# General pass in steps of 128 tokens, cut into finer parts; the first q block by rows; the second group's weight maxima later

## The chip, the cores and the metric

One core of a Trainium2 chip runs the whole program. Its engines are TensorE (PE in the rows, PEld its weight loads), VectorE (DVE), ScalarE (ACT), GpSimd (POOL) and SyncE (SP), whose queue issues nearly all the transfers. The metric is the device time of one execution in microseconds; the median of three runs is compared.

## The reference, cut to what matters

```python
# attention over pooled keys, four batches of 12288 tokens, 128 channels
kv_pool = kv.reshape(B, H // 4, 4, W // 4, 4, C).mean(axis=(2, 4))
k = v = kv_pool.reshape(B, -1, C) @ w_sr              # 768 keys per batch
s = (q @ k.transpose(0, 2, 1)) / np.sqrt(C)
a = np.exp(s - s.max(-1, keepdims=True))
x = (a / (a.sum(-1, keepdims=True) + 1e-9)) @ v
# top-1 mixture of 8 experts, 128 -> 1024 -> 128
logits = x @ w_gate
e = argmax(logits)                                     # per token
y = np.maximum(x @ w1[e], 0) @ w2[e] * softmax(logits)[e]
```

q is drawn with a standard deviation of 0.8, the other inputs are small, so that within a batch nearly all tokens choose the same expert.

## The kernel before, in words

The tokens go in 96 blocks of 512 (24 per batch), in groups of four blocks (the first group of batch 0 has two). For a block the kernel takes scores in four tiles of 128 tokens (`scores`: six matmuls, a row maximum `nmax` on VectorE, the exponential `a` on ScalarE, a split into two f16 halves `ah`, a DMA transpose to `aT`), then the values (`values`, 18 matmuls), the split `xh`, `xl`, and the logits. For a group it counts votes and takes the expert that most tokens chose; all its blocks run through that expert. The expert part has eight slices `f` of the hidden layer: three matmuls into a PSUM bank (`hidden_sum`), the relu `hh` on ScalarE, the rest `hl` on VectorE, which frees the bank, and three slices later the three matmuls into `y` (`combine`). A product is always the sum of three with split operands.

A token that chose another expert than its group isn't covered. `code` notes it, `left` counts such tokens by (batch, expert), and a general pass serves them: `count_steps` turns the counts into steps of TAIL tokens, and `tail_step` is one step for one (batch, expert) list. It works out which list and which part of it (`u`, `li`), loads that expert's weights and that batch's keys and values, counts the list's tokens along each partition (`hit`, `tab`), finds the rows of each tile of 128 (`sel`, `row`, `v`, `at`), gathers their q rows by an indirect DMA, splits the weights, and then runs scores, values, gate and the expert part on TAIL columns; `tail_rows` writes the rows back by one indirect DMA per tile. With TAIL = 256 a step has TC = 2 tiles. Two steps (EXTRA) are placed between the last block but one and the last block; a loop at the end would run further ones. `tail_step` is a generator: it yields between its parts, and `search()` advances every running step by one part; it is called once behind each slice `f` of the last blocks (`m_`). A second step starts when the first has set `found`.

Most of the program is ordered by hand. `at(time, part, ...)` puts a part on a list by a due time in units near a microsecond, `beside(t, c, ...)` hangs one on the score matmuls of block t, tile c, and `run` emits the parts in the order of their times; each engine works through its own parts in that order. The first eight blocks have a shorter plan (`plan_short`, SHORT = 9.8 a block), the others LEN = 18.7, with the expert part LAG = 8 blocks behind. `plan_group` places a group's gate and votes and `plan_weights` its weights: `scales_part` advances `weight_scales` (two maxima over the weights on VectorE, `ws` L407, a matmul, then the scales), `split_part` the f16 halves. The second group has its own branch (`t < LAG`). The last eight blocks and the general steps stand outside this: they are written in program order, of which the framework may depart.

At the start `kv_load` issues four transfers for each of six key tiles, `first_keys` pools them (`pooled` on VectorE, eight matmuls that add the other half on TensorE), projects them and, at the last tile but one, prepares the first block's q: it was loaded in 32-column pieces (`q_load`, four transfers), turned on VectorE in blocks of 32 x 32 (`q_turn`), copied to `qh` on ScalarE, with the rest `ql` on VectorE.

Of the kernel before, what the change touches and what calls it, by code (L numbers as in the profile page):

```python
# [10 lines left out]
F32 = mybir.dt.float32  # L11
# [8 lines left out]
P = 128  # L20
# [10 lines left out]
TINY = 1e-30  # L31
TAIL = 256
EXTRA = 2
# [5 lines left out]
def attention_moe(ctx: ExitStack, tc, q, kv, w_sr, w_gate, w1, w2, out, tail=True):  # L39
    nc = tc.nc  # L40
# [6 lines left out]
    KT = NK // P  # L47
# [480 lines left out]

    def q_prep(t):
        q_turn(t)  # L530
        q_high(t)
        q_low(t, nc.vector)

    pending, waiting, searches = [], [], []
# [200 lines left out]
    def tail_step(job, aside=False):  # L735
# [6 lines left out]
        nc.vector.tensor_mul(le, le, ends)  # L742
        nc.vector.tensor_reduce(u[:, 1:2], le, axis=AX.X, op=ALU.max)
        nc.vector.tensor_sub(u[:, 1:2], step, u[:, 1:2])
        nc.vector.tensor_scalar_mul(u[:, 1:2], u[:, 1:2], float(TAIL))
# [20 lines left out]
        nc.vector.tensor_scalar(hit[:, :NJ], code, u[:, 2:3], None, op0=ALU.is_equal)  # L766
        nc.vector.tensor_tensor_scan(tab[:, :NJ], hit[:, :NJ], hit[:, :NJ], 0.0, op0=ALU.add, op1=ALU.max)
        nc.vector.tensor_copy(tab[:, NJ + 1:NJ + 2], part)
        nc.vector.memset(tab[:, NJ + 2:NJ + 3], 1.0)
        yield  # L770
        yield
        cnt = tab[:, NJ - 1:NJ]
# [8 lines left out]
        for c in range(TC):  # L781
# [11 lines left out]
            row = one.tile([P, NJ + 3], F32, name="row")  # L793
            nc.vector.tensor_copy(row, pr[:, :NJ + 3])

            nc.vector.tensor_scalar(v[:, 2:3], part, u[:, 1:2], float(c * P), op0=ALU.add, op1=ALU.add)
# [18 lines left out]
        for _ in weight_scales(raw, to, bank):  # L815
            pass
        ws = to[0]
        for _ in split_expert(raw, ws, w, 0, aside):
            pass
        yield  # L820
        for _ in split_expert(raw, ws, w, 1, aside):
            pass
        job["found"] = True
        yield
        pq = bank()
# [21 lines left out]
        job["x"] = x = xh, x_low(po, k, TAIL, xh)  # L847
        yield
        yield
# [35 lines left out]
    raws = {}  # L885
    for t in range(KT):
        raws[t] = kv_load(0, t)
        if t == KT - 3:
            q_load(0, nc.sync)
    q_load(1, nc.sync)  # L890
    gate_weights()

    def first_keys():

        for t in range(KT):
            kv_pool(0, t, raws.pop(t))
            pt = bank()[:, :P]
            k = KEYS[0]
            own = k.pop(("pooled", t))
            parts = k.pop(("parts", t))  # L900
            for i, part_ in enumerate(parts):
                mm(pt, part_, ident, i == 0, False)
            if t > 0:
                kv_project(0, t - 1, bank()[:, :P])
                kv_high(0, t - 1)
            mm(pt, own, ident, False, True)
            k["pt"] = pt
            kv_turned(0, t)
            if t > 0:
                kv_low(0, t - 1)  # L910
            if t == KT - 2:
                q_prep(0)
        kv_project(0, KT - 1, bank()[:, :P])
# [123 lines left out]
    def plan_group(g, t):  # L1037

        if t < LAG:

            T = LAG * LEN
            group_gate(g)
            for _ in range(6):
                at(T + 3.5, gate_part, g)
# [6 lines left out]
            at(T + 15.0, gate_part, g)  # L1051
            return plan_weights(g, t + 1)
        T = t * LEN
# [16 lines left out]

    def plan_weights(g, t):
        T = t * LEN
        at(T + 17.1, scales_part, g)
        T += LEN
        at(T + 0.7, scales_part, g)
        beside(t + 1, 1, scales_part, g)
        at(T + 5.8, scales_part, g)
        at(T + 6.8, gate_part, g)
        at(T + 6.85, gate_part, g)
        at(T + 9.25, split_part, g, 0)  # L1080
        at(T + 14.95, split_part, g, 0)
# [200 lines left out]
```

## Time and profile before

| | |
|---|---|
| median of 3 runs (lowest, highest) | 1928.78 us (1925.33, 1931.13) |
| profiled execution: time, span | 1929.05 us, 1927.3 us |
| TensorE busy | 1875.2 us (97%) |
| VectorE busy | 1419.7 us (74%) |
| ScalarE busy | 1306.2 us (68%) |
| GpSimd busy | 1365.6 us (71%) |
| mean granted clock of TensorE | 0.994 of full speed |

The shares are means over stages with different limits. A matmul's busy time overlaps its neighbours', so the distance between two starts is the better measure of what one costs.

### The profile page before, as it was taken

Reading aid. Unit: us, or ns where it says so; the run is one execution under the profiler, and the core shown is the slowest. Engines: PE = TensorE matmul, PEld = TensorE weight load, DVE = VectorE, ACT = ScalarE, POOL = GpSimd, SP = SyncE. Lnnn points to the kernel's source line nnn. Section 1 sums busy time; section 2 is a strip of 40 time slices with the busy share of each in tenths; the row PEclk is TensorE's granted clock in tenths of the full one; section 3 lists DMA queues with packets and bytes.
Section 4 is the critical chain, followed back from the end, with each engine's and each line's share of the span. In section 5 each row is a group of like instructions: output and inputs, shape, how many; then the busy total and the mean of one; then the engine's idle time right before and its main releaser. Section 6 shows DMA issues by size and latency. Waiting matters only on the chain.

```text
span 1927.3 us, 30394 instructions
## 1 busy us (share of the span) xinstructions
PE 1875.2 (97%) x9950; PEld 1095.0 (57%) x9950; DVE 1419.7 (74%) x2774; ACT 1306.2 (68%) x2376; POOL 1365.6 (71%) x1395
## 2 busy tenths in 40 slices
PE   6889999999999999999999999999999999999987
PEld 5655555555555555555555555555555555555444
DVE  5777787877787787776777777767767767767685
ACT  2777767766776766766767767767667677677454
POOL 1778688668878867867778787678677677776253
PEclk8999999999999999999999999999999999999999
DMA  6888989769987976887878777877867777776432
GB/s 163 164 165 160 186 168 174 145 126 191 177 165 152 189 146 123 172 153 130 178 156 173 167 152 143 157 136 159 147 129 143 150 126 147 143 135 132 112 95 46
DMA packets 1001409, 287.85 MB, mean 149 GB/s; under 512 B 905984, under 2 KB 983938, under 8 KB 1001248
## 3 DMA queue, kind: packets, MB, share of 16 engines
q1 hardware_dynamic: 1000992, 285.79, 75.2%
q8 instruction: 79, 1.29, 0.3%
q14 instruction: 82, 0.67, 0.1%
q0 software_dynamic: 256, 0.10, 0.0%
HBM read 81.34 MB, written 30.15 MB: 58 GB/s over the span
## 4 chain that ended last, share of the span: by engine, by line
PE 88%; DVE 4%; DMA 3%; issue 2%; POOL 1%; ACT 1%; SPq 1%; POOLq 0%; DVEq 0%; ACTq 0%
PE m L131 44%; PE y L131 25%; PE s L131 20%; DVE hl L460 1%; DMA aT<-ah 1%; DMA kv_raw<-in_kv_dram 1%; POOL ah L338 1%; SPq L173 0%; DMA aT<-in_kv_dram 0%; DVE nmax L309 0%; ACT a L313 0%; ACT hh L454 0%; DVE ws L407 0%; DMA kv_raw<-in_moe_w_dram 0%; DMA yT<-y 0%
## 5 line engine op out<-in xcount | busy, mean ns | idle before, releaser
L338 POOL TENSOR_TENSOR ah<-a,ah 128x768 f16<-128x768 f32 x381 | 626.0, 1647 | 313.0 <-ACT ah L336 297.8
L454 ACT ACTIVATE hh<-m 128x512 f16<-128x512 f32 (+1 forms) x784 | 462.6, 591 | 412.3 <-PE m L131 410.6
L460 DVE SCALAR_TENSOR_TENSOR hl<-m,hh 128x512 f16<-128x512 f32 (+1 forms) x784 | 532.7, 681 | 227.6 <-ACT hh L454 199.2
L131 PE MATMUL s<-k_sb,qh 128*128 128x384 f32 x1552 | 469.9, 383 | 4.7 <-ACT a L313 4.5
L313 ACT ACTIVATE a<-s,nmax 128x768 f32<-128x768 f32 x388 | 350.5, 903 | 125.9 <-DVE nmax L310 104.9
L309 DVE TENSOR_REDUCE nmax<-s 128x1 f32<-128x768 f32 x388 | 369.6, 953 | 68.2 <-PE s L131 60.0
L131 PE MATMUL m<-aT,v_sb 128*128 128x512 f16 (+1 forms) x1656 | 383.6, 377 | 1.6 <-DVE hl L460 1.6
L131 PEld LDWEIGHTS s<-k_sb,qh 128*128 128x128 f32 x1552 | 288.0, 190 | 61.7 <-ACT a L313 6.7
L131 PE MATMUL m<-xh,w1h 128*128 128x512 f16 (+1 forms) x776 | 296.3, 382 | 13.0 <-DVE hl L460 10.3
L131 PE MATMUL y<-hh,w2h 128*128 128x512 f16 (+1 forms) x776 | 293.6, 378 | 1.8 <-ACT y L483 1.8
L131 PE MATMUL y<-hl,w2h 128*128 128x512 f16 (+1 forms) x776 | 293.9, 379 | 0.0
L131 PE MATMUL y<-hh,w2l 128*128 128x512 f16 (+1 forms) x776 | 293.9, 379 | 0.0
L131 PE MATMUL m<-xl,w1h 128*128 128x512 f16 (+1 forms) x776 | 293.7, 378 | 0.0
L131 PE MATMUL m<-xh,w1l 128*128 128x512 f16 (+1 forms) x776 | 293.4, 379 | 0.0
L131 PEld LDWEIGHTS <-v_sb 128*128 128x128 f16 x1764 | 170.9, 98 | 204.3 <-issue 3.8
L131 PE MATMUL s<-k_sb,ql 128*128 128x384 f32 x776 | 262.8, 339 | 0.6 <-DVE ql L295 0.6
L131 PEld LDWEIGHTS <-w2h 128*128 128x128 f16 x1552 | 151.5, 98 | 184.0 <-issue 6.7
L334 POOL CAST ah<-a 128x768 f16<-128x768 f32 x187 | 154.3, 825 | 85.6 <-ACT a L313 80.7
L131 PEld LDWEIGHTS <-w1h 128*128 128x128 f16 x1552 | 124.6, 100 | 136.6 <-issue 62.0
L336 ACT CAST ah<-a 128x768 f16<-128x768 f32 x194 | 161.9, 834 | 9.5 <-issue 3.6
L354 DVE SCALAR_TENSOR_TENSOR xl<-m,xs,xh 128x512 f16<-128x512 f32 (+1 forms) x92 | 68.6, 745 | 129.2 <-ACT xh L349 127.3
L527 POOL TENSOR_TENSOR ql<-qT,qh 128x512 fp32r<-128x512 f32 x95 | 120.9, 1272 | 48.5 <-ACT qh L522 48.3
(214 smaller groups left out, 2087.7 us busy)
## 6 DMA issues: line engine op xcount, KB each, us to landing
kv_raw<-in_moe_w_dram SPq DMA_DIRECT2D x54, 512.0 KB, 4.7
q_sb<-in_q_dram SPq DMA_DIRECT2D x384, 64.0 KB, 2.5
out_dram<-o SPq DMA_DIRECT2D x96, 256.0 KB, 2.3
kv_raw<-in_kv_dram SPq DMA_DIRECT2D x84, 256.0 KB, 4.6
aT<-ah SPq DMA_TRANSPOSE x381, 3.8
aT<-in_kv_dram SPq DMA_DIRECT2D x12, 256.0 KB, 7.4
k_dram<-k_sb SPq DMA_DIRECT2D x8, 384.0 KB, 3.1
v_dram<-v_sb SPq DMA_DIRECT2D x8, 192.0 KB, 2.6
```

What stands on the lines that cost most here:

```text
L131: nc.tensor.matmul(o, l, r, start=start, stop=stop)
L309: nc.vector.tensor_reduce(nmax, pss[:, :, :KH], axis=AX.XY, op=ALU.max, negate=True)
L313: nc.scalar.activation(a.rearrange("p (h k) -> p h k", h=2), pss[:, :, :KH], AF.Exp, bias=nmax, scale=1.0, accum_out=sums)
L334: nc.gpsimd.tensor_copy(ah[:, 0], a)
L336: nc.scalar.copy(ah[:, 0], a)
L338: nc.gpsimd.tensor_sub(ah[:, 1], a, ah[:, 0])
L354: nc.vector.scalar_tensor_tensor(xl[:, :n], po[:, :n], k["xs"][:, 0:1], xh[:, :n], op0=ALU.mult, op1=ALU.subtract)
L454: nc.scalar.activation(hh[:, :n], ph[:, :n], AF.Relu)
L460: nc.vector.scalar_tensor_tensor(hl[:, :n], ph[:, :n], 0.0, hh[:, :n], op0=ALU.max, op1=ALU.subtract)
L527: by.tensor_sub(ql, BL[t].pop("qT"), qh)
```

## The change

TAIL becomes 128, so a general step has one tile. `tail_step` yields at other places: more often among its first VectorE instructions, after each part of the weights' maxima and of their split, and no longer at places where nothing was done. The first block's q is loaded by whole rows in one transfer, ahead of the last key tile, turned by four TensorE transposes into a PSUM bank, and split from there. For the second group the first part of the gate is placed earlier, and the two weight maxima and what follows them later.

```diff
--- before.py
+++ after.py
@@ -29,7 +29,7 @@
 W1_TOP = 2.0 ** 5
 W_TOP = 2.0 ** 14
 TINY = 1e-30
-TAIL = 256
+TAIL = 128
 EXTRA = 2
 SQ = 32
 FAR = 1.0e6
@@ -526,11 +526,6 @@
         qh, ql = BL[t]["qhl"]
         by.tensor_sub(ql, BL[t].pop("qT"), qh)
 
-    def q_prep(t):
-        q_turn(t)
-        q_high(t)
-        q_low(t, nc.vector)
-
     pending, waiting, searches = [], [], []
     OTHERS = {}
 
@@ -741,6 +736,7 @@
         nc.vector.tensor_reduce(u[:, 0:1], le, axis=AX.X, op=ALU.add)
         nc.vector.tensor_mul(le, le, ends)
         nc.vector.tensor_reduce(u[:, 1:2], le, axis=AX.X, op=ALU.max)
+        yield
         nc.vector.tensor_sub(u[:, 1:2], step, u[:, 1:2])
         nc.vector.tensor_scalar_mul(u[:, 1:2], u[:, 1:2], float(TAIL))
         nc.vector.tensor_scalar_add(u[:, 2:3], u[:, 0:1], 1.0)
@@ -765,10 +761,9 @@
         nc.vector.tensor_scalar(below, slot, part, None, op0=ALU.is_gt)
         nc.vector.tensor_scalar(hit[:, :NJ], code, u[:, 2:3], None, op0=ALU.is_equal)
         nc.vector.tensor_tensor_scan(tab[:, :NJ], hit[:, :NJ], hit[:, :NJ], 0.0, op0=ALU.add, op1=ALU.max)
+        yield
         nc.vector.tensor_copy(tab[:, NJ + 1:NJ + 2], part)
         nc.vector.memset(tab[:, NJ + 2:NJ + 3], 1.0)
-        yield
-        yield
         cnt = tab[:, NJ - 1:NJ]
         pb = bank()
         mm(pb[:, :1], below, cnt, True, True)
@@ -792,6 +787,7 @@
             mm(pr[:, :NJ + 3], sel, tab[:, :NJ + 3], True, True)
             row = one.tile([P, NJ + 3], F32, name="row")
             nc.vector.tensor_copy(row, pr[:, :NJ + 3])
+            yield
 
             nc.vector.tensor_scalar(v[:, 2:3], part, u[:, 1:2], float(c * P), op0=ALU.add, op1=ALU.add)
             nc.vector.tensor_sub(v[:, 2:3], v[:, 2:3], row[:, NJ:NJ + 1])
@@ -813,15 +809,12 @@
         w = job["w"] = []
         to = []
         for _ in weight_scales(raw, to, bank):
-            pass
+            yield
         ws = to[0]
-        for _ in split_expert(raw, ws, w, 0, aside):
-            pass
-        yield
-        for _ in split_expert(raw, ws, w, 1, aside):
-            pass
         job["found"] = True
-        yield
+        for i in range(2):
+            for _ in split_expert(raw, ws, w, i, aside):
+                yield
         pq = bank()
         for c in range(TC):
             nc.tensor.transpose(pq[:, c * P:(c + 1) * P], q_sb[:, c, :], ident)
@@ -846,7 +839,6 @@
         xh = x_high(po, k, TAIL)
         job["x"] = x = xh, x_low(po, k, TAIL, xh)
         yield
-        yield
         lg = one.tile([P, TC, E], F32, name="lg_t", bufs=2)
         logits_sum(logits(x, TC, bank()), lg)
         to = []
@@ -884,9 +876,11 @@
 
     raws = {}
     for t in range(KT):
+        if t == KT - 1:
+
+            q0 = two.tile([P, CH, C], F32, name="q_sb")
+            nc.sync.dma_start(q0, q[0, :BLK].rearrange("(c p) d -> p c d", p=P))
         raws[t] = kv_load(0, t)
-        if t == KT - 3:
-            q_load(0, nc.sync)
     q_load(1, nc.sync)
     gate_weights()
 
@@ -909,7 +903,10 @@
             if t > 0:
                 kv_low(0, t - 1)
             if t == KT - 2:
-                q_prep(0)
+                pq = bank()
+                for c in range(CH):
+                    nc.tensor.transpose(pq[:, c * P:(c + 1) * P], q0[:, c, :], ident)
+                BL[0]["qhl"] = q_halves(pq, CH, nc.vector)
         kv_project(0, KT - 1, bank()[:, :P])
         kv_high(0, KT - 1)
         kv_low(0, KT - 1)
@@ -1040,7 +1037,8 @@
 
             T = LAG * LEN
             group_gate(g)
-            for _ in range(6):
+            at(begin(LAG - 1) + 4.64, gate_part, g)
+            for _ in range(5):
                 at(T + 3.5, gate_part, g)
             at(T + 6.1, group_count, g)
             beside(LAG, 2, group_votes, g)
@@ -1049,7 +1047,7 @@
             at(T + 12.35, gate_part, g)
             at(T + 12.4, group_left, g)
             at(T + 15.0, gate_part, g)
-            return plan_weights(g, t + 1)
+            return plan_weights(g, t + 1, True)
         T = t * LEN
         group_gate(g)
         at(T + 6.8, gate_part, g)
@@ -1068,16 +1066,16 @@
         at(T + 15.0, gate_part, g)
         plan_weights(g, t + 1)
 
-    def plan_weights(g, t):
+    def plan_weights(g, t, late=False):
         T = t * LEN
-        at(T + 17.1, scales_part, g)
+        at(T + (18.9 if late else 17.1), scales_part, g)
         T += LEN
-        at(T + 0.7, scales_part, g)
-        beside(t + 1, 1, scales_part, g)
-        at(T + 5.8, scales_part, g)
+        at(T + (5.8 if late else 0.7), scales_part, g)
+        beside(t + 1, 2 if late else 1, scales_part, g)
+        at(T + (11.4 if late else 5.8), scales_part, g)
         at(T + 6.8, gate_part, g)
         at(T + 6.85, gate_part, g)
-        at(T + 9.25, split_part, g, 0)
+        at(T + (11.55 if late else 9.25), split_part, g, 0)
         at(T + 14.95, split_part, g, 0)
         at(T + 16.8, split_part, g, 0)
         at(T + 18.9, split_part, g, 1)
```

`q_halves`, which the new lines call, copies the PSUM bank to `qh` on ScalarE and subtracts it to `ql` on the engine that it is given.

## Rows read from the trace of the kernel before

**Rows 1.** The page: span, and the queue of the indirect transfers (packets, MB, share).
```profile
span 1927.3 us, 30394 instructions
...
q0 software_dynamic: 256, 0.10, 0.0%
```

**Rows 2.** Busy time of each engine by stage; then granted clock, DMA share, GB/s.
```profile
150.00:1790.00 1640.00, 1640.00 (x8683) 947.75 (x8681) 1215.96 (x2300) 1150.18 (x2082) 1232.58 (x1258) 1.00 0.79 153
...
1816.00:1860.00 44.00, 34.31 (x149) 15.84 (x148) 40.80 (x112) 24.57 (x39) 24.27 (x29) 0.97 0.56 164
...
1882.00:1906.00 24.00, 20.11 (x148) 13.88 (x147) 16.28 (x42) 14.69 (x34) 12.05 (x12) 1.00 0.36 78
1906.00:1918.00 12.00, 11.65 (x59) 5.58 (x56) 6.41 (x11) 5.41 (x10) 3.02 (x3) 1.00 0.02 5
```

**Rows 3.** SyncE's queue of transfers near the start, in order of time.
```profile
13.94 3.66 SPq L514 DMA_DIRECT2D q_sb<-in_q_dram  x4
```

**Rows 4.** All engines where the first keys end, in order of time.
```profile
31.12 0.69 DVE L527 TENSOR_TENSOR ql<-qT,qh 128x512 fp32r<-128x512 f32 x1 [0.69 <-ACT qh L522]
...
31.73 1.88 DVE L181 TENSOR_REDUCE pooled<-kv_raw 128x128 f32<-128x1024 f32 x1
...
34.82 0.60 PE L131 MATMUL s<-k_sb,qh 128*128 128x384 f32 x2
...
35.10 0.28 ACT L218 ACTIVATE k_sb<-m 128x128 fp32r<-128x128 f32 x1 [0.58 <-PE m L131]
...
35.57 0.29 DVE L224 SCALAR_TENSOR_TENSOR k_sb<-m,k_sb 128x128 fp32r<-128x128 f32 x1 [1.57 <-ACT vT L219]
```

**Rows 5.** TensorE around the second group; brackets give the wait and what ended it.
```profile
123.70 0.38 PE L131 MATMUL m<-xh,w1h 128*128 128x512 f16 x1 [1.48 <-DVE hl L460]
...
138.11 0.38 PE L131 MATMUL m<-xh,w1h 128*128 128x512 f16 x1 [2.33 <-DVE lg L367]
```

**Rows 6.** VectorE in the same stretch.
```profile
118.69 1.10 DVE L379 TENSOR_SCALAR gate<-sums 128x16 f32<-128x16 f32 x1
...
136.12 1.22 DVE L407 TENSOR_REDUCE ws<-kv_raw 128x1 f32<-128x1024 f32 x1 [2.31 <-DMA kv_raw<-in_moe_w_dram]
```

**Rows 7.** TensorE groups by shape, 1815 to 1928 us.
```profile
L131 PE MATMUL m<-vT,sel 128*128 128x387 f32 x8 | 4.1, 602 | 0.1
```

**Rows 8.** The chain that ended last: six score matmuls of a general step.
```profile
1851.79 1.06 PE s L131 x6
```

**Rows 9.** TensorE in the second general step: neighbouring 256-column matmuls.
```profile
1905.00 0.27 PE L131 MATMUL m<-xl,kv_raw 128*128 128x256 f16 x1
1905.11 0.27 PE L131 MATMUL m<-xh,kv_raw 128*128 128x256 f16 x1
```

**Rows 10.** TensorE in a logits stretch: neighbouring pairs, each with its weight load.
```profile
1793.96 0.17 PE L131 MATMUL m<-wg,xh 128*128 128x16 f16 x1
1793.98 0.17 PE L131 MATMUL m<-wg,xl 128*128 128x8 f16 x1
```

**Rows 11.** Who waited for whom on TensorE, 1790 to 1928 us: total, times, longest.
```profile
PE m L131 <- DVE hl L460: 11.4, 12, 4.0
```

**Rows 12.** VectorE groups by shape, 1815 to 1928 us.
```profile
L786 DVE TENSOR_TENSOR v<-v,vT 128x1 f32<-128x1 f32 x4 | 2.3, 585 | 0.0
...
L806 DVE TENSOR_SCALAR at<-v 128x1 int32<-128x1 f32 x4 | 0.6, 149 | 0.1
```

**Rows 13.** All engines at the end, in order of time.
```profile
1916.81 0.97 POOL L871 DMA_INDIRECT out_dram<-o,at  x1 [4.64 <-DVE o L500]
...
1919.02 0.69 DVE L500 TENSOR_TENSOR o<-m,cover 128x512 f32<-128x512 f32 x1 [2.49 <-PE m L498]
1919.15 0.97 POOL L871 DMA_INDIRECT out_dram<-o,at  x1 [1.37 <-DMA out_dram<-o,at]
1923.03 0.37 SPq L721 DMA_DIRECT2D out_dram<-o  x1
```

**Rows 14.** Busy time by stretch after the longest wait of the tail.
```profile
1857.00:1864.00 7.00, 6.02 (x14) 2.37 (x14) 4.99 (x11) 1.19 (x2) 2.71 (x3) 0.52 0.59 114
```

## Prediction

> **What bounds the kernel now.** I read the stages first. From 150 to 1790 us TensorE is busy for all 1640.00 of 1640.00 us [rows 2], and the diff changes nothing that is issued there; so this stretch keeps its length and only slides with whatever ends before it. What can move lies at the two ends. In the tail, from 1816 on, the picture turns: between 1816 and 1860 VectorE is busy 40.80 of 44 us and TensorE only 34.31 [rows 2], so there the search of the general steps on VectorE sets the pace. The waits of TensorE say how: 12 waits of 11.4 us in all end at `hl`, the longest 4.0 us [rows 11]; `hl` frees the PSUM bank that the next hidden matmul needs, and it stands on VectorE's queue behind pieces of the search. From 1882 to 1918 TensorE works 20.11 + 11.65 of 36 us [rows 2]: short waits, mostly its own work. At the start the transfer queue and VectorE's order decide, and near 136 us one stall can be read off directly.
>
> **Is the number of steps the same?** A step serves one (batch, expert) list. The indirect queue moved 0.10 MB in both directions [rows 1]; at 512 B a row that is at most 0.105 MB / 2 / 512 B, about 103 rows each way, pad rows not moved. So no list can hold more than 128 rows, every list that fitted one step of 256 fits one of 128, and the closing loop, of which the trace shows no pass, stays empty. Both placed steps remain, at half the width.
>
> **The yields.** I counted the calls of `search()` that a step needs: before, 12 to `found` and 26 to the end; after, again 12 and 26. A step begins and ends at the same places of the block program; only the work inside is cut finer. The weight load moves from the second call to the third and its maxima from the eleventh to the ninth, six calls later instead of nine; a call comes once per part of a block, six 512-column matmuls of twice 0.109 us [rows 9], so six calls are some 8 us. If the load is issued late all the same, the maximum waits in front of an `hl`, as it does for 2.31 us near 136 [rows 6], and TensorE behind it; I leave that to the range.
>
> **Tail, TensorE.** Two 256-column matmuls start 0.109 us apart [rows 9]. No 128-column f16 matmul with its own weight load stands in the trace. Bounds: 0.109 (no gain) and 0.02, at which pairs of 8 and 16 columns start, each behind a weight load [rows 10]. I take half, 0.055, since 256 columns are five times as slow as the floor and columns therefore set the pace. Per step 48 matmuls of the expert and 18 of the values shrink: 2 x 66 x 0.054 = 7.1 us. One score tile per step goes, 1.06 each [rows 8]: 2.1. One `sel` matmul pair per step goes: four tiles took 4.1 us busy [rows 7], overlapped, so 0.8 each: 1.6. The turns of q and of the output and the logits of the second tile, a few tenths: 0.3. Sum 11.1 us. Against it: one f takes six matmuls, 0.33 us, nearly what ScalarE (0.28) and VectorE (0.29) need for 128 columns [rows 4]; TensorE no longer covers them with ease, so I give back 1.0 (bounds 0 and 3). Net 10.1.
>
> **Tail, VectorE.** Twelve groups make one tile's search; their means, from 585 ns down to 149 [rows 12], sum to 4.96 us. One tile per step disappears, 9.9 us over both steps, besides a row maximum each. TensorE's waits between 1816 and 1860 are 44 - 34.31 = 9.7 us [rows 2]; with the search's clumps halved and the two weight maxima and the split no longer in one piece, I take 3.0 of them back (bounds 0 and 9.7): part of a removed clump only uncovers the wait for ScalarE. Behind the longest wait the granted clock was 0.52 for 7 us [rows 14], so TensorE's 6.02 us there were near its lower level, 1.2 GHz, and would have taken about 3.1 at 2.4; if that wait falls short, up to 2.9 returns. I take 1.2.
>
> **The end.** Now two indirect writes of the last step follow each other, and the last block's output waits for both: its data are ready at 1919.02 + 0.69 = 1919.71, its transfer is issued at 1923.03 [rows 13], 3.3 us later. The second write started 2.34 behind the first, at 1919.15, and the output 3.88 behind the second [rows 13]: a write takes 2.3 to 3.9 us to land. A single one from 1916.81 lands between 1919.1 and 1920.7. Gain 2.3 to 3.3, taken 2.9.
>
> **Start.** The first q load goes: four transfers that held the queue for 3.66 us [rows 3]. One transfer in whole rows takes their place, moved on SyncE's queue past the four transfers of the last key tile but one, ahead of the last four. Its bytes are the same, so the last keys gain at most 3.66 less one issue of a quarter of it, 2.7, at least nothing. On VectorE the turn goes, and `ql` (which waited 0.69 for ScalarE) still stands in front of the last `pooled`, 31.73 to 33.61, behind which the scores start at 34.82 [rows 4]. New wait: TensorE's four turns need q, and behind them on TensorE stand the last tile's sums, on VectorE `ql` and the last `pooled`. q is issued ahead of the last keys, so it lands first, and the turns, at most 0.3 us each by the score row [rows 4], fall where TensorE waits for keys anyway; without that cover they cost 1.2. Bounds of the gain: 1.0 (only the turn and its wait) to 3.5; I take 2.5. The ramp behind it is placed relative to its own events, so it slides.
>
> **Second group.** VectorE waited 2.31 us for weights and then ran the maximum, 1.22 [rows 6]; behind it stood `hl` and `lg`, and TensorE waited 2.33 us for `lg` [rows 5]. Placed 1.8 units later, the maximum stands behind both, and the weights have landed by then: that wait goes to nobody. Next behind it is the next block's row maximum; before, both weight maxima stood ahead of it, now one, so it isn't later. The first gate part (1.10 us [rows 6]) leaves a row of gate work ahead of an `hl` for which TensorE waited 1.48 [rows 5]: up to 1.4. The second maximum now stands ahead of an `hl` in the next block: up to 1.2 lost. Bounds 0.4 to 3.8, taken 2.5.
>
> **Sum.** 10.1 + 3.0 + 1.2 + 2.9 + 2.5 + 2.5 = 22.2 us. The profiled execution took 1929.05 us (span 1927.3 [rows 1], 1.75 around it), the median of three runs is 1928.78, so the base is the same. 1929 - 22 = 1907.
>
> **Rivals.**
> - *The clumps dissolve.* If all of the 9.7 us and of the clock's 2.9 come back instead of 3.0 and 1.2, another 8.4 us go: 1898. For it: VectorE is the bound there by its busy time. Against: some `hl` waited for ScalarE, which keeps its work.
> - *The tail follows the chain of the search.* Then matmul time turns into waits: the 7.1 us of narrower matmuls, less the 1.0 given back, and the 3.0 and 1.2 of the waits and the clock don't come: 1907 + 10 = 1917. For it: 34.31 of 44 [rows 2]. Against: 11.65 of 12 at the very end.
> - *Weight loads set the pace of half-width matmuls.* If a 128-column matmul waits for its weights, the step between two starts comes near the 256-column one, and of 7.1 us little stays, say 1.5: 1912.6. Against: pairs with their loads 0.02 us apart [rows 10].
>  The Trainium skill, "TensorE: Matmul & The Clock Gate", section "Back-to-back issue gap", says that in streams of weight load and matmul the loads count too, and gives 81 ns at 128 columns; by that estimate the saving would be 132 x 0.028 = 3.7 us, and the time 1910. By that rule this rival gets a chance of its own; the rows of the logits pairs speak against it.
> - *No change.* A later wait of the ramp takes back the 2.5 and 2.5 of start and second group, the 10.1 and 4.2 of the tail turn into waits for the search, and only the end's 2.9 stays: 1926. For it: the second tile's search hangs between the same placed parts. Against: no later wait for a transfer shows on TensorE after 150 [rows 2], which works there without a gap.
> - *Slower: the clock.* From the first general step on, half-width steps leave TensorE waiting for ScalarE and VectorE, and it falls to 1.2 GHz as after 1857 [rows 14]. Each microsecond of work then costs another. After 1882 some 31.8 us of work stand [rows 2], 24 when the halved part is off; the forecast turns over once more than 22 us of them run at the lower level: 1931. For it: it happened once. Against: that took a wait of 4.0 us, and the last block's full-width work, 11.65 of 12 us [rows 2], follows the steps.
>
> **Chances.** Forecast 0.50, clumps dissolve 0.18, chain of the search 0.16, weight loads 0.08, no change 0.05, slower 0.03. The first four end faster by more than 0.3% (5.8 us, about what a measurement of this kernel can tell): 0.92; same 0.05; slower 0.03. Range: from 1897, just past the dissolved clumps, to 1918, just past the chain of the search; the forecast's own lies within, 1901 to 1913, from the bounds of its larger terms taken half way.
>
> **What would show it.** Scores of the first block near 32.3 instead of 34.82; no wait for `lg` near 135; 128-column matmuls 0.055 apart in the two steps; waits for `hl` after 1790 at 8 us or less in all; one indirect write per step and the last output issued within a microsecond of its data. Wrong would be a stretch of low clock after the steps, a new TensorE wait for q's turns, or a wait for the weight maxima, which now come six calls after the load.

## The result and the profile after

The changed kernel takes 1910.73 us (median of 4, 1909.15 to 1911.63), the kernel before 1929.95 (median of 4, 1925.33 to 1931.88): ratio 0.9903 [0.9883, 0.9923]. A second comparison gave 1913.25 (5 runs) against 1929.99 (11 runs), ratio 0.9913 [0.9900, 0.9925]. The forecast was 1907, a gain of 22.2 us; the two comparisons gave 19.2 and 16.7, so 3 to 6 us of it did not come. The rows below are of the changed kernel's profiled execution (1910.12 us).

**Steps.** The page: its span, and the indirect queue with half of its packets, as in [rows 1] the same bytes.
```profile
span 1908.3 us, 30286 instructions
...
q0 software_dynamic: 128, 0.10, 0.0%
```
One gather and one write per step are left (two of each in the trace); both steps run in their places, and the closing loop makes no pass.

**Start.** TensorE where the first keys end, in order of time; brackets give the wait and what ended it.
```profile
24.87 0.60 PE L908 MATMUL m<-ident,q_sb 128*128 128x128 f32 x4
27.16 2.05 PE L131 MATMUL m<-ident,kv_raw 128*128 128x128 f32 x16 [1.69 <-DMA kv_raw<-in_kv_dram]
30.38 0.59 PE L131 MATMUL s<-k_sb,qh 128*128 128x384 f32 x2
```
The turns of q cause no wait of their own, TensorE waits for keys behind them, and the scores start at 30.38 instead of 34.82 [rows 4]. These 4.44 us are one execution's: "again", below, shows that they must not be read as the edit's gain.

**Second group.** TensorE's wait, then VectorE's two maxima.
```profile
118.53 0.38 PE L131 MATMUL m<-xh,w1h 128*128 128x512 f16 x1 [0.63 <-DVE hl L460]
```
```profile
131.46 1.22 DVE L407 TENSOR_REDUCE ws<-kv_raw 128x1 f32<-128x1024 f32 x1 [0.51 <-DMA kv_raw<-in_moe_w_dram]
...
137.00 1.21 DVE L407 TENSOR_REDUCE ws<-kv_raw 128x1 f32<-128x1024 f32 x1
```
The wait of 1.48 [rows 5] is 0.63, that of 2.33 is gone; VectorE still waits 0.51 for the weights, with nobody behind it who is late.

**Body.** The same row maximum in block 11 and in block 95 (the third of each block), first of before, then of after.
```profile
185.17 0.96 DVE L309 TENSOR_REDUCE nmax<-s 128x1 f32<-128x768 f32 x1 [0.48 <-PE s L196]
...
1770.75 0.96 DVE L309 TENSOR_REDUCE nmax<-s 128x1 f32<-128x768 f32 x1 [0.37 <-PE s L131]
```
```profile
178.22 0.96 DVE L309 TENSOR_REDUCE nmax<-s 128x1 f32<-128x768 f32 x1 [0.49 <-PE s L196]
...
1766.06 0.96 DVE L309 TENSOR_REDUCE nmax<-s 128x1 f32<-128x768 f32 x1 [0.38 <-PE s L131]
```
From the one to the other 1585.58 us pass before and 1587.84 after. A stretch in which no instruction changed has become 2.26 us longer; TensorE is idle for 0.04 us of it after and never before, and its granted clock is 1.00 in both. The prediction had this at nothing.

**Tail.** I measure it from the same logits matmul, behind block 95's row maxima, to the start of the last `y` matmul: one row of before, one of after.
```profile
1777.45:1917.27 139.82, 125.35 (x651) 63.94 (x650) 101.49 (x255) 75.49 (x135) 60.09 (x73) 0.98 0.36 89
```
```profile
1772.78:1900.45 127.67, 114.68 (x628) 56.88 (x626) 85.98 (x227) 70.73 (x131) 52.44 (x66) 0.97 0.38 91
```
TensorE is busy 125.35 and 114.68 us, idle 14.47 and 12.99. Part of the busy time is the low clock's: before, 6.02 us at 0.52 [rows 14], 2.9 us more than at full speed; after, two stretches:
```profile
1849.00:1851.00 2.00, 2.00 (x7) 1.47 (x6) 0.57 (x1) 0.60 (x1) 0.00 (x0) 0.50 0.00 0
1851.00:1853.00 2.00, 2.00 (x7) 0.97 (x6) 1.03 (x2) 0.60 (x1) 0.00 (x0) 0.67 0.00 0
1883.00:1885.00 2.00, 2.00 (x25) 1.99 (x23) 0.73 (x4) 0.60 (x2) 1.43 (x3) 0.51 0.00 0
1885.00:1887.00 2.00, 2.00 (x26) 2.00 (x25) 1.61 (x10) 1.16 (x5) 1.04 (x1) 0.64 0.01 2
```
That is 2 x (0.50 + 0.33 + 0.49 + 0.36) = 3.4 us. So the work at full speed fell from 122.5 to 111.3, by 11.2 us; the idle time fell by 1.5; the clock cost 0.5 more. The split repeats: work at full speed is 122.3 to 122.6 us in the four profiles with the old step (before, start_only, group_only, rows_old_place) and 111.1 to 111.3 in the four with the changed one (after, again, old_layout, layout_on); the low clock costs 1.5 to 2.9 us (mean 2.2) in the former and 3.1 to 3.4 (mean 3.3) in the latter. The columns' part can be seen in the distance between two starts of 128-column matmuls:
```profile
1888.31 0.22 PE L131 MATMUL y<-hh,kv_raw 128*128 128x128 f16 x1
1888.36 0.22 PE L131 MATMUL m<-xh,kv_raw 128*128 128x128 f16 x1
1888.42 0.22 PE L131 MATMUL m<-xl,kv_raw 128*128 128x128 f16 x1
```
TensorE's waits in the tail, by what ended them (total, times, longest; two smaller ones, 0.6 and 0.5, left out):
```profile
PE m L131 <- DVE hl L460: 5.1, 6, 2.0
PE y L131 <- ACT y L483: 2.4, 3, 1.0
PE m L131 <- DMA aT<-ah: 1.7, 1, 1.7
PE y L131 <- ACT hh L454: 0.9, 1, 0.9
PE m L131 <- DVE sel L784: 0.8, 1, 0.8
PE y L131 <- DVE hl L460: 0.8, 1, 0.8
```
The hidden matmuls' waits for `hl` halved, from 11.4 [rows 11] to 5.1 (6.4 with those of other matmuls for `hl`); all other lines together took 2.4 us in this stretch before and take 7.7 now.

**End.** GpSimd's write, the last output's data, its transfer.
```profile
1899.96 0.98 POOL L863 DMA_INDIRECT out_dram<-o,at  x1 [6.97 <-DVE o L500]
1902.20 0.69 DVE L500 TENSOR_TENSOR o<-m,cover 128x512 f32<-128x512 f32 x1 [2.51 <-PE m L498]
1902.91 0.37 SPq L716 DMA_DIRECT2D out_dram<-o  x1
```
The transfer is issued 0.02 us after its data (1902.89) instead of 3.3 us [rows 13]. From the last `y` matmul to the span's end it takes 7.85 us; before, 1927.3 - 1917.27 = 10.03.

### The profile page after: what moved, and what is told of

Read it like the earlier page. It is cut to its first block, busy times and chain, and to the rows that moved or that the text cites. A ratio compares the mean times of both kernels' runs of the same rounds, so it can differ in the third digit from the quotient of the medians.

```text
span 1908.3 us, 30286 instructions
## 1 busy us (share of the span) xinstructions
PE 1865.3 (98%) x9930; PEld 1089.2 (57%) x9930; DVE 1402.6 (73%) x2745; ACT 1301.6 (68%) x2372; POOL 1358.7 (71%) x1387
## 4 chain that ended last, share of the span: by engine, by line
PE 90%; DVE 5%; DMA 2%; ACT 2%; issue 1%; POOL 0%; SPq 0%; ACTq 0%; DVEq 0%; POOLq 0%
PE m L131 44%; PE y L131 25%; PE s L131 20%; DVE hl L460 1%; DVE nmax L309 1%; DMA kv_raw<-in_kv_dram 1%; DVE ws L407 1%; ACT a L313 1%; DMA aT<-ah 1%; ACT hh L454 0%; DMA aT<-in_kv_dram 0%; ACT ah L336 0%; SPq L173 0%; POOL ah L338 0%; DMA kv_raw<-in_moe_w_dram 0%
## 5 line engine op out<-in xcount | busy, mean ns | idle before, releaser
L489 POOL COPY o<-yT 128x512 uint16<-128x512 uint16 x190 | 136.9, 768 | 34.7 <-DMA yT<-y 34.6
```

The source lines that it names most:

```text
L489: nc.gpsimd.tensor_copy(o.bitcast(U16).rearrange("p c (d i) -> p i c d", i=2)[:, i], yT.rearrange("p (i c) d -> p i c d", i=2)[:, i])
```

## The experiments

One execution's spread is several microseconds (the kernel before, on one chip: 1923.75 to 1930.58 in 27 runs). In part it goes with the mean granted clock of the execution: on that chip 1923.75 and 1924.26 us at 0.997, 1927.11 and 1930.06 at 0.993, but 1924.71 to 1930.58 at 0.995; in the second comparison 1925.21 to 1927.16 at 0.996 and 0.997, 1929.19 to 1931.63 at 0.995 and below. So times here are medians and ratios, differences from the kernel before are worked out from the ratio, and single stretches of a profile are used where they repeat: the tail of the changed kernel measured 127.67 and, in "again", 127.69 us.

**start_only**: the kernel before with the first q block by rows.
```
+        if t == KT - 1:
+            q0 = two.tile([P, CH, C], F32, name="q_sb")
+            nc.sync.dma_start(q0, q[0, :BLK].rearrange("(c p) d -> p c d", p=P))
         raws[t] = kv_load(0, t)
-        if t == KT - 3:
-            q_load(0, nc.sync)
...
-                q_prep(0)
+                for c in range(CH):
+                    nc.tensor.transpose(pq[:, c * P:(c + 1) * P], q0[:, c, :], ident)
+                BL[0]["qhl"] = q_halves(pq, CH, nc.vector)
```


> The kernel before with the first q block by rows alone (new load, new place, turn on TensorE); general steps and second group as before. Theory (the parts add up): the first scores start near 30.4 us instead of 34.8, and these 4.4 us reach the end: about 4.4 us below the kernel before, ratio 0.9977. Rival (the block loop takes part of any lead back, as the last blocks of the changed kernel led by 4.7 where block 11 led by 7.0): the lead shrinks by 1 to 2.4 us between block 11 and block 90, ratio 0.9985 to 0.9990.

Measured: 1924.41 us (11 runs) against 1927.55 (27 runs), ratio 0.9986 [0.9977, 0.9995], 2.7 us less (1.0 to 4.4 by the interval). Its profile starts the scores at 30.10. The time is the rival's, not its reason: from block 11 to block 95 the lead over the kernel before shrinks by 0.3 us only. The 4.4 us of the theory were one pair of executions ("again", below).

**group_only**: the kernel before with the second group's gate part and weight maxima moved.
```
-            for _ in range(6):
+            at(begin(LAG - 1) + 4.64, gate_part, g)
+            for _ in range(5):
                 at(T + 3.5, gate_part, g)
...
-            return plan_weights(g, t + 1)
+            return plan_weights(g, t + 1, True)
```


> The kernel before with the second group's gate part and weight maxima moved alone. Theory (the parts add up): the waits of 1.48 and 2.33 us near 123 and 136 us go and 2.7 us reach the end, ratio 0.9986. Rival (the stall went in the changed kernel because the start had made room for the weights): the weights land as late as before against TensorE's work, VectorE waits for them at the new place too, and less than 1 us is left, ratio 0.9995 or more.

Measured: 1924.51 us (11 runs), ratio 0.9987 [0.9978, 0.9996], 2.5 us less (0.8 to 4.2), as the theory had it. The wait of 2.33 for `lg` is gone, one of 1.40 for `hl` stays.

**narrow_only**: the kernel before with half-width steps, in the old parts.
```
-TAIL = 256
+TAIL = 128
```


> The kernel before with general steps of 128 tokens alone, the old cut of their parts. Theory (the narrower work is the gain, the finer cut adds little): the 11 us of TensorE work and some 2 us at the end go, the waits stay as long in sum as in the changed kernel: 13 to 15 us below the kernel before, ratio 0.9922 to 0.9933. Rival (the finer cut carries part of it, since it takes the maxima and the splits apart): with the old cut the waits for hl stay above 8 us and the gain is 8 to 11 us, ratio 0.994 to 0.996.

Measured: 1920.74 us (11 runs), ratio 0.9972 [0.9963, 0.9981], 5.4 us less (3.7 to 7.1), under both ranges that were expected. Its profile is of the fastest of the eleven executions (1918.36 us, clock 0.995; mean of the eleven 0.9937, of the kernel before on that chip 0.9949), so it shows more of a gain than the median. Its tail takes 130.26 us, 9.6 less than before's, with TensorE idle for 16.6 us instead of 14.5: the width took the work away, and part of the time turned into single long waits, seen in the table of waits:
```profile
PE m L131 <- DVE hl L460: 7.7, 10, 1.8
PE m L131 <- DVE sel L789: 2.8, 1, 2.8
PE m L131 <- DVE ws L407: 1.7, 2, 1.0
PE m L131 <- DMA aT<-ah: 1.6, 1, 1.6
PE m L131 <- DVE gate L379: 1.4, 1, 1.4
```
Its body, from block 11's to block 95's row maximum, takes 1587.53 us, 1.95 longer than before's, in start_only 1585.84. So the loss in the body comes with the width.

The three parts add up to 10.6 us by these ratios. The changed kernel without the finer cut (coarse_cut, below) gained 13.7, on another chip; with intervals of 1.7 us to either side of each part the difference stays within the noise.

**rows_old_place**: the q block by rows, its transfer left at the old place in the queue (one run).
```
-        if t == KT - 3:
-            q_load(0, nc.sync)
+        if t == KT - 3:
+            q0 = two.tile([P, CH, C], F32, name="q_sb")
+            nc.sync.dma_start(q0, q[0, :BLK].rearrange("(c p) d -> p c d", p=P))
```


> The kernel before with the first q block loaded by whole rows in one transfer at the old place (ahead of the last two key tiles) and turned on TensorE. If the form of the load and the turn bring the start's gain, the last keys land as in the changed kernel and the first scores start at 30.4 to 30.9 us. If the new place brings it, the last keys land as before and the first scores start at 32 us or later, only the turn on VectorE saved.

Measured: 1925.18 us; the scores start at 30.86, 0.76 behind start_only's. That is within what the start varies by. So this execution starts early without the new place, and what the place alone is worth stays open.

**again**: the changed kernel once more.

> The changed kernel itself once more, so that the other three stand beside it on one chip: 0.9903 of before, some 1910.7 us, as in the first comparison. Its body should lose about 2 us of its lead over before between blocks 11 and 95 again, if that loss belongs to the kernel; if it belonged to one execution, it will be absent.

Measured: 1913.25 us, ratio 0.9913; the body takes 1587.09 us, 1.5 more than before's. Its start, as TensorE's rows show it:
```profile
29.97 2.90 PE L131 MATMUL m<-ident,kv_raw 128*128 128x128 f32 x16 [2.37 <-DMA kv_raw<-in_kv_dram]
34.46 0.60 PE L131 MATMUL s<-k_sb,qh 128*128 128x384 f32 x2
```
```profile
31.00:35.00 4.00, 3.57 (x18) 3.19 (x17) 0.48 (x2) 0.96 (x5) 0.00 (x0) 0.58 0.42 66
```
The same program starts its scores at 30.38 in one execution and at 34.46 in another: the last keys came 2.8 us later, and the sums over them took 2.90 instead of 2.05. The last row shows why the sums took longer: the granted clock was 0.58 from 31 to 35 us, where it was 1.00 in the changed kernel's first profile. Over all profiles here, the first scores start at 34.82, 33.58 and 33.64 with the old start (mean 34.01) and at 30.10 to 34.46 in ten executions with the new one (mean 31.55; rows_old_place left out): 2.5 us. At block 7's third row maximum the means are 110.85 and 108.31, the same 2.5.

**coarse_cut**: the changed kernel with the step's parts cut as before (the diff's hunk of `tail_step` undone, but for the width).
```
             nc.vector.tensor_copy(row, pr[:, :NJ + 3])
-            yield
...
         for _ in weight_scales(raw, to, bank):
-            yield
+            pass
         ws = to[0]
+        for _ in split_expert(raw, ws, w, 0, aside):
+            pass
+        yield
+        for _ in split_expert(raw, ws, w, 1, aside):
+            pass
         job["found"] = True
...
```


> The changed kernel with the old cut of the general step: step 128 wide, start and second group as changed, but the parts of the search as before. Theory 1, the finer cut matters: in the profiles TensorE idles 16.6 us between the last full block's logits and the last matmul with the narrow step alone, 13.0 with all of the change; the difference of 3.6 us is what the cut brings, so this kernel takes 3.6 us longer than the changed one, 1914.3, with single TensorE waits for sel, ws and the gate above 1 us. Theory 2, the cut is worth nothing and the idle time follows the narrow width alone: 1910.7, like the changed kernel.

Measured: 1916.15 us (6 runs), ratio 0.9929 [0.9918, 0.9941], 2.9 us above "again". The intervals of the two ratios overlap; the tail's row, against 127.69, does not leave it open:
```profile
1774.88:1907.18 132.30, 115.59 (x628) 56.37 (x626) 87.40 (x227) 71.44 (x131) 51.88 (x66) 0.96 0.36 88
```
TensorE is idle for 16.7 us, 3.7 more than with the finer cut, as theory 1 said, with `hl` 9.1, `sel` 3.0, `ws` 1.7 and the gate 1.2; the other 0.9 of the 4.6 us is busy time, where the low clock costs 4.6 instead of 3.4.

**old_layout**: the changed kernel, its small tiles as large as for 256 tokens.
```
-            at = one.tile([P, 1], I32, name="at", bufs=2 * TC)
+            at = one.tile([P, 1], I32, name="at", bufs=4)
...
-        sums = one.tile([P, TC], F32, name="sums_t", bufs=2)
+        sums = one.tile([P, 2], F32, name="sums_t", bufs=2)
...
-        lg = one.tile([P, TC, E], F32, name="lg_t", bufs=2)
+        lg = one.tile([P, 2, E], F32, name="lg_t", bufs=2)[:, :TC]
...
-        sc = job["scale"] = one.tile([P, TC], F32, name="scale_t", bufs=2)
+        sc = job["scale"] = one.tile([P, 2], F32, name="scale_t", bufs=2)[:, :TC]
```


> The changed kernel, in which four small tiles of the general step (row numbers, sums, logits, scales) keep the size that they had for 256 tokens, so that every tile allocated behind them (keys, values, q, a, aT, xh) lies 128 bytes further on, where it lay before. No instruction differs. Theory 1, the place of the tiles in SBUF costs the 0.03 to 0.05 us per block by which the narrow kernels' blocks are longer: the lead over before at block 95 stays near the 7.0 us of block 11 instead of 4.7, and the time falls by some 2 us, to 1908.7. Theory 2, the loss comes of something else (the program's length, its place in memory): the lead falls by 2 us all the same, 1910.7.

Measured: 1911.19 us (5 runs), ratio 0.9895 [0.9880, 0.9910], 2.1 us below "again", whose interval overlaps this one; the trace decides: the tail takes 127.57 us as ever, and the body:
```profile
180.93 0.96 DVE L309 TENSOR_REDUCE nmax<-s 128x1 f32<-128x768 f32 x1 [0.48 <-PE s L196]
...
1766.74 0.96 DVE L309 TENSOR_REDUCE nmax<-s 128x1 f32<-128x768 f32 x1 [0.37 <-PE s L131]
```
1585.81 us, 0.23 more than before's. Theory 1 holds: where the tiles lie sets the length of the body.

The traces also show which work grows. From block 11 to block 95 the six score matmuls of a tile (`s<-k_sb,qh` and `s<-k_sb,ql`), from their first start to the next matmul's, take 1.240 to 1.242 us in the mean in the seven kernels whose tiles lie at the old place, and 1.244 to 1.245 in the seven in which they lie elsewhere. The f16 matmuls of 512 columns start 0.216 to 0.217 us apart in all fourteen. With four tiles in each of 84 blocks, 0.0045 us a tile is 1.5 us (an estimate from these means), most of the loss.

**search_earlier**: the second step's search may begin three calls earlier.
```
+        job["found"] = True
         w = job["w"] = []
         to = []
         for _ in weight_scales(raw, to, bank):
             yield
         ws = to[0]
-        job["found"] = True
```


> The changed kernel, with the second step's search allowed to begin as soon as the first step's rows are requested, three calls earlier, ahead of the first step's weight maxima. Theory 1, what is left idle in the tail is the latency of the second step's chain (its values waited 1.75 us for the transposed scores, and TensorE's clock was 0.51 for some 4 us behind that wait): the wait goes, the low clock with it, and 2 to 3.5 us are saved, 1907.2 to 1908.7. Theory 2, VectorE's load in the tail is the bound: the two searches overlap more, the waits for hl grow by what the other wait loses, and the time stays at 1910.7 or rises by up to 2 us.

Measured: 1910.26 us (5 runs), ratio 0.9901 [0.9888, 0.9914], 3.0 us below "again", with intervals that overlap. The profile is of the fastest of the five (1906.53 us). Its tail, and two of its waits:
```profile
1772.78:1896.74 123.96, 111.91 (x628) 54.58 (x626) 87.67 (x227) 70.86 (x131) 52.23 (x66) 1.00 0.38 94
```
```profile
PE m L131 <- DVE hl L460: 5.4, 8, 2.0
PE m L131 <- DMA aT<-ah: 1.8, 1, 1.8
```
The size is theory 1's, its mechanism is not: the wait for the transposed scores stayed, at 1.8 us. What went is the low clock (1.00 throughout), so that TensorE's busy time fell by 2.8 us, and 0.9 us of idle time. Theory 2 falls too: all waits for `hl` together grew by 1.1 us only (6.4 to 7.5), and those for ScalarE's `y` and `hh` shrank by more.

**layout_on**: as old_layout, with the logits tile of four columns (`[P, 4, E]`), so that all behind it lies 128 bytes past the old place (one run).

> The changed kernel with the tiles behind the general step's small ones 256 bytes further on, 128 bytes past the place that they had before. Theory 1, what counts is where a tile lies within 256 bytes: then this kernel is like the changed one, and its lead over before shrinks by some 2 us between blocks 11 and 95. Theory 2, the changed kernel's place alone is bad, or the distance to another tile: the lead stays within 0.3 us, as with the old place.

Measured: 1911.65 us; the body takes 1587.68 us, as long as the changed kernel's. So 128 bytes to either side of the old place cost the same 2 us, which agrees with theory 1. Three places are too few to say that 256 bytes are the period.

**weights_cut**: coarse_cut with the weights' part alone cut finer (one run).
```
         for _ in weight_scales(raw, to, bank):
-            pass
+            yield
...
-        for _ in split_expert(raw, ws, w, 0, aside):
-            pass
-        yield
-        for _ in split_expert(raw, ws, w, 1, aside):
-            pass
+        for i in range(2):
+            for _ in split_expert(raw, ws, w, i, aside):
+                yield
```


> The kernel with the old cut of the step at 128 tokens (132.3 us from the last full block's logits to the last matmul, TensorE waiting 16.6 us in it) with the finer cut of the weights alone: one call for each maximum and each piece of the split. Theory 1, VectorE's weight maxima in one piece are what hurts: the waits for ws (1.7 us) and most of the 4 us by which the waits for hl exceed the changed kernel's go, and the stretch takes some 128 us. Theory 2, the search's own pieces hurt (sel 3.0 us, gate 1.2 us): those waits stay, and the stretch takes 130.5 us or more.

Measured: 1913.89 us; the tail takes 131.83 us. By the sum theory 2 is nearer, but its waits are not what stayed: `sel`, `ws` and the gate went, and one other came, by the table of waits (TensorE is idle for 16.6 us, as with the old cut):
```profile
PE m L131 <- DVE hl L460: 8.0, 11, 2.2
PE m L131 <- DMA aT<-ah: 4.0, 1, 4.0
```
The wait moved along the chain to the transposed scores. So the weights' part alone doesn't carry the finer cut's gain; the search's parts alone were not run.

**both**: old_layout and search_earlier together.

> The changed kernel with the two edits that helped: the tiles behind the general step's small ones lie where they lay before, and the second step's search begins three calls earlier. Theory 1, the two gains are in different places (blocks 11 to 95; the low clock in the tail) and add: some 1.8 to 2.1 us and 2.3 to 3.0 us below the changed kernel, ratio to before near 0.988, and the stretch from the last full block's logits to the last matmul takes 124 us with the clock at 1.00. Theory 2, the early search was only lucky in its one traced execution: that stretch takes 127.6 us again and the ratio is that of the layout alone, 0.9895.

Measured: 1906.23 us (4 runs) against 1928.46 (6 runs), ratio 0.9887 [0.9869, 0.9904]; body 1586.03, tail 123.94 us. Theory 1: both gains are there in the profile. With both_later, below, it is the best version run, 3 to 5 us below the changed kernel by its ratio, though the intervals overlap.

**both_later**: "both" with three more empty calls ahead of the second step's values.
```
-        for _ in range(5):
+        for _ in range(8 if aside else 5):
             yield
```


> As the one before, with three more empty calls between the second step's scores and its values, so that the values stand where they stood in the changed kernel, while the scores come three calls earlier. Theory 1, the wait of 1.8 us for the transposed scores is the latency of that transfer chain counted in calls: it goes, the stretch from the last full block's logits to the last matmul takes 122.2 us, and the time is 1.8 us below the kernel with five empty calls. Theory 2, TensorE has nothing else to do there: the wait moves to the next thing the second step needs (its gate, its hidden sums), and the time stays.

Measured: 1906.60 us (4 runs), ratio 0.9883 [0.9865, 0.9900], the same as "both": theory 2 by the time. The wait for the transposed scores fell to 1.0, the waits of `y` for `hl` rose from 0.8 to 2.0. The tail took 125.26 us, 1.7 of which are a low clock behind a wait far ahead of the edit. That wait in "both" and in "both_later", and the clock behind it:
```profile
1819.93 0.38 PE L131 MATMUL m<-xh,w1h 128*128 128x512 f16 x1 [1.95 <-DVE hl L460]
```
```profile
1820.00:1822.00 2.00, 2.00 (x12) 0.99 (x12) 2.00 (x4) 0.60 (x1) 0.00 (x0) 1.00 1.24 308
1822.00:1824.00 2.00, 2.00 (x12) 0.97 (x11) 1.62 (x13) 0.85 (x2) 0.81 (x2) 1.00 0.84 220
```
```profile
1819.83 0.38 PE L131 MATMUL m<-xh,w1h 128*128 128x512 f16 x1 [1.95 <-DVE hl L460]
```
```profile
1820.00:1822.00 2.00, 2.00 (x9) 0.95 (x8) 1.96 (x4) 0.60 (x1) 0.00 (x0) 0.76 1.20 305
1822.00:1824.00 2.00, 2.00 (x7) 1.03 (x6) 1.31 (x12) 0.00 (x0) 1.00 (x2) 0.50 0.88 245
```
The same wait of 1.95 us is followed by 2.4 GHz in the one execution and by 1.2 GHz in the other. So the clock's part of search_earlier's gain is not secured by its trace alone; "both" showed it a second time. The clock of all executions agrees: its mean is 0.9953 over the nine of the changed kernel (0.994 to 0.997), 0.9970 over search_earlier's five and 0.9973 over the eight of "both" and "both_later" (all 0.996 to 0.998). Of some 1910 us the difference of 0.0017 to 0.0020 is 3.2 to 3.8 us, an estimate from these means.

## Why the prediction was right, and where it was not

Direction and range held, and so did the mechanism of the larger terms: less work on TensorE in the general steps, an earlier start, no wait for `lg`, one write at the end. Two terms came out with the wrong sign, the body and the clock. Term by term (us gained):

| term | forecast | measured |
|---|---|---|
| start | 2.5 | 2.5 (means of 10 and 3 executions) |
| second group | 2.5 | 2.4 (below) |
| body, "keeps its length" | 0 | -1.5 to -2.3 |
| tail, TensorE's work | 11.1 | 11.2 |
| tail, waits: 3.0 taken back, 1.0 given | 2.0 | 1.5 |
| tail, clock | 1.2 | -0.5 |
| the end | 2.9 | 2.2 |
| sum | 22.2 | 17.0 to 17.8 |

The two comparisons gave 19.2 and 16.7 us, 14.9 to 22.6 and 14.5 to 19.3 by their intervals; the sum lies in both.

- *Start.* The size was right; the 4.44 us of the first trace would have made the bound of 3.5 look wrong. How much of it belongs to the place in the queue was not settled.
- *Second group.* From block 7's to block 11's row maximum the ten kernels with this edit gain 1.6 to 2.8 us, mean 2.4. The wait that the second maximum might have caused in the next block doesn't show.
- *The failed step: "this stretch keeps its length and only slides".* TensorE is busy for all but 0.04 us of it in both kernels, so the page and the table of waits show nothing; only the distance between equal instructions does. The width of the step shrinks four small tiles, the tiles behind them move by 128 bytes, and blocks grow by up to 0.05 us (18.18 to 18.23 in blocks 82 and 86). The growth is not even: 1.24 of the 2.26 us fall in blocks 67 to 95. old_layout takes it back. Most of it stands at the score matmuls, as the means behind old_layout show; why these take longer stays open.
- *Tail, work.* 11.1 against 11.2, and matmuls of 128 columns 0.055 us apart, as forecast (mean of 24 distances near 1888 us). The rival "weight loads set the pace" falls with it. The Trainium skill, "TensorE: Matmul & The Clock Gate", section "Back-to-back issue gap", gives 81 ns for this stream at 128 columns; here each of these matmuls has its own weight load, and the trace shows 55, so the measurement decides.
- *Tail, waits.* The `hl` waits fell as said, below 8 us, and the net came to 1.5, not 2.0. That has a wider reason than the forecast's wait for ScalarE: the chain of the search came next as well. coarse_cut and weights_cut show it: take one wait out, and the next link (`sel`, `ws`, the gate, the transposed scores) waits for nearly as long. The width alone makes idle time (14.5 to 16.6), the cut takes it down (13.0). The rivals "clumps dissolve" (9.7 us back) and "the tail follows the search" (the narrower work lost) are both refuted by the split into work and idle time.
- *Tail, clock.* The other term that failed, with the wrong sign: the prediction let the low clock go with the longest wait. That wait fell from 4.0 to 2.0 us, yet two stretches at 1.2 GHz took the place of one, and they do not stand behind the longest wait:
```profile
1821.00 0.38 PE L131 MATMUL m<-xh,w1h 128*128 128x512 f16 x1 [1.95 <-DVE hl L460]
1848.59 0.38 PE L131 MATMUL m<-xh,w1h 128*128 128x512 f16 x1 [1.77 <-DVE hl L460]
```
```profile
1821.00:1823.00 2.00, 2.00 (x10) 1.01 (x10) 2.00 (x4) 0.60 (x1) 0.00 (x0) 1.00 1.21 311
```
Behind the wait of 1.95 the clock stays at 1.00, behind that of 1.77 it is 0.50, and behind the wait of 1.75 for the transposed scores it is 0.51; the same two stretches show in "again", old_layout and layout_on. Of the signs of being wrong that the prediction named, this one came in part: a stretch of low clock in the second step, 1.7 us of loss, far from the 22 that would have turned the forecast over. By the means of the four profiles each above, the term is -1.1.
- *The end.* The output no longer waits, as said; the issue came 3.3 us nearer to the data, the upper bound. But from the issue to the span's end it took 1.1 us longer (5.39, before 4.27), which leaves 2.2. That is not this one execution's: it took 4.3 to 4.5 us in the four kernels with the old step and 5.0 to 5.9 in the ten with half-width steps. From the last `y` matmul to the span's end the means are 9.9 and 7.9, a gain of 2.0. So 2.9 was too much because part of the wait came back in the transfer; why stays open.

## What to carry to other kernels

Split a stretch into work at full clock, idle time and clock before comparing: here the work came to a tenth of a microsecond as counted, while most of the idle time only changed its owners. Making a tile smaller moves every tile allocated behind it, so compare the distance between equal instructions in stretches that "did not change", and keep the old sizes if it grew. Don't read a gain at the start of a kernel off one pair of executions.

## What the runs showed of the hardware

- The place of tiles in SBUF changes the pace of a stretch in which TensorE hardly idles: 1585.6 to 1586.6 us from block 11 to 95 in the seven kernels whose tiles behind the small ones lie at the old place, 1587.1 to 1587.8 in the seven in which they lie 128 bytes to either side. Less TensorE's idle time there (0 to 0.4 us) it is 1585.6 to 1586.2 and 1587.1 to 1587.8. The six score matmuls of a tile take 1.240 to 1.242 us in the former and 1.244 to 1.245 in the latter.
- The granted clock behind one and the same wait of 1.95 us was 1.00 in one execution ("both") and 0.50 in another (both_later); a wait of 1.8 us left it at 1.00 in search_earlier, where the changed kernel's wait of 1.75 us was followed by 0.51.
- The last of the first keys of one program arrived 2.8 us apart in two executions, and the scores behind them started 4.1 us apart; in the later one the granted clock was 0.58 on the way.
- The time of one execution goes in part with its mean granted clock: 1923.75 and 1924.26 us at 0.997, 1927.11 and 1930.06 at 0.993, for the kernel before on one chip.
- The last output's transfer took 4.3 to 4.5 us from its issue to the span's end where it had waited for two indirect writes of a step, and 5.0 to 5.9 where it followed its data at once behind one.
